# Memory attention with a gated feed-forward: two of four key and value chunks kept in q's buffers, phi's products in one piece beside P's last block

## The chip, the cores and the metric

One Trainium2 chip, one core. The metric is the device time of one launch in microseconds. All arithmetic that the text speaks of is in float32, or in float32 split into a high part (rounded to the chip's fp32r format) and a low part, so that most products are made three times: high by high, high by low, low by high.

## What is computed

Eight batches, eight heads, 576 tokens, head width 64, 32 memory slots per head; then a feed-forward network over all 4608 tokens.

```
a = softmax(phi, axis=2)                     # over the 576 tokens, phi[b, h, s, 32]
k_m = einsum('bhsm,bhsd->bhmd', a, k)        # 32 memory keys per head
v_m = einsum('bhsm,bhsd->bhmd', a, v)
attn = softmax(q @ k_m^T / 8, axis=-1)       # over the 32 slots
x = (attn @ v_m), heads side by side         # [4608, 512]
out = silu(x @ w_in) @ w_out                 # 512 -> 2048 -> 512
```

## The kernel before

**Blocks and slots.** The work goes batch by batch; a batch is called a block here, `b` from 0 to 7. `x @ w_in` is not made as such: attn (576 tokens by 256 head-and-slot pairs) is multiplied with P = v_m @ w_in, which has to be made anew for each block (`p_mm`, four pieces of 512 columns, `JW`). Blocks 2 to 7 run in 16 slots, `s = 8t + j`: token half `t` (288 tokens), and a pair `j` of 128-row chunks of the hidden layer. In each slot TensorE makes `h` (`ffn1s`, L836, twelve products into a PSUM tile of two banks), then small pieces of work for this or the next block (called by `run`), then the second layer's 21 products of the slot before (`st_step`, L875, into four banks `sum`). The second layer is a seven-product form of the 2 by 2 block product, for which `forms` builds sums of silu's output: ScalarE does silu (L850, and L852 for the 64 left columns) and the high parts (L854, L864), VectorE the sums (L855, L858, L859) and the low parts (L865, L866). In one slot of the first half VectorE does some of ScalarE's share (L861, L862), because ScalarE has an exp there.

**The next block's attention.** While block `b` runs, the pieces for block `n = b + 1` are put into slots by `ev(b, slot, fn, ...)`; `steady` does it for blocks 2 to 6. With `ex` = 4 in block 2 and 2 in blocks 3 to 6: `phi_exp` in slot `ex` (ScalarE, L319, with a load of the exp table before it and of the silu table behind it), `e_mm` (phi's products with keys and values, TensorE, L335: 16 products for each of four chunks of 128 tokens, and L345: 8 more and 8 more for the 64 tokens that are left), `e_tr`, then `s_all` (the scores, slot `ex + 5`, reads q). `e_mm` ends with the division by phi's sum: two additions and two reciprocals on VectorE (L353, L355), then one half of the result scaled on ScalarE (L359) and the other on VectorE (L361), both read from PSUM. In blocks 3 to 6, `p_mm` of P's third quarter stands in slot 0 and of its last quarter in slot 2; its result is read by ScalarE (`p_split`, L659) and VectorE (L661). In slot 3 there is also half of the softmax's scaling on VectorE (`s_norm`, L444), and in blocks of odd number the last three additions of the second layer of the block before (L916).

**PSUM.** Eight banks: four for `sum`, two for `h` (one tile, `bufs=1`, so that the next slot's `h` waits until everything that reads the tile is done), two for `bg`, which the small pieces use in turn. `h` fills columns 0 to 287 of each of its banks. `beside_h(w)` gives the `w` columns behind these, in the tile of the slot's own `h`.

**Homes in SBUF.** From block 3 on only two of the four chunk buffers `kv0` to `kv3` are left for keys and values, since the other two hold forms of `w_out`. So chunks 2 and 3 are loaded into `kv0` and `kv1` after the first half of `e_mm` has read these, and `e_mm` is made in two pieces, two slots apart (slots `ex + 1` and `ex + 3`). q has two buffers of its own, `q0` and `q1`, a little larger than a chunk (4608 to 4128 bytes a partition), filled by `load_q` and read by `s_all`.

**What sets the order.** TensorE runs in the order in which the code is written, and so does ScalarE from block 1 on. VectorE and the DMA queue (SyncE's, here SP) are ordered by a scheduler, under constraints: in a slot, VectorE's work that comes from `run` stands behind the slot's last `forms` instruction and behind `p_split`'s VectorE instruction (`behind`). DMAs are issued by SP in its order; each waits at the head of the queue until its buffer is free.

Of the kernel before, what the change touches and what calls it, by code (L numbers as in the profile page):

```python
# [10 lines left out]
F32 = mybir.dt.float32  # L11
# [8 lines left out]
P = 128  # L20
B, S, H, M, D = 8, 576, 8, 32, 64
HM = H * M
NR = H // 2
KVW = 2 * D + 1
# [3 lines left out]
JW = 512  # L28
# [6 lines left out]
FULLC = S // P  # L35
# [13 lines left out]
def attn_ffn_kernel(  # L49
# [11 lines left out]
    sb = ctx.enter_context(tc.tile_pool(name="sb", bufs=2))  # L61
# [53 lines left out]
    def bgtile():  # L115
        return ps.tile([P, 2, 512], F32, tag="bg", name="bg", bufs=1)
# [90 lines left out]
    at = [dict() for _ in range(B)]  # L207
    live = {}

    def banks(b):  # L210
        if b == 0:
            return [ps.tile([P, 512], F32, tag="acc", name=f"first{i}", bufs=NI) for i in range(2)]
        bg = bgtile()
        return [bg[:, 0], bg[:, 1]]

    def beside_h(w):

        return [live["h"][:, i, HALF : HALF + w] for i in range(2)]
# [10 lines left out]
    def load_kv(b, cs=range(FULLC)):  # L229
        queue = nc.scalar if b == 0 else None  # L230
        ts = at[b].setdefault("kv", [])
        for c in cs:
            n = c if b < 3 else c % 2
            t = sb.tile([P, 2, NR, KVW], F32, tag=f"kv{n}", name=f"kv{b}_{c}", bufs=1)
            load(t.rearrange("p g r f -> p (g r f)"), kv[b, :, c * KVC : (c + 1) * KVC], queue=queue)
            ts.append(t)
        if cs[0]:
            return
        t = sb.tile([P, NR, KVW], F32, tag="kr", name=f"kr{b}", bufs=1)
        load(t.rearrange("p r f -> p (r f)"), kv[b, :, FULLC * KVC :], queue=queue)  # L240
        at[b]["kr"] = t
# [6 lines left out]
    def rows(p):  # L248
        return slice(REST * p, REST * (p + 1))
# [75 lines left out]
    def e_mm(b, cs=range(FULLC)):  # L325
        e, er, kvt, kr = (at[b][k] for k in ("e", "er", "kv", "kr"))
        if cs[0] == 0:
            at[b]["pt"] = beside_h(KVW) if b == 2 else banks(b)
        pt = at[b]["pt"]
        turns = [(c, p) for c in cs for p in range(2)]  # L330
        if b == 0:
            turns.sort(key=lambda t: t[1])
        for c, p in turns:
            for r in range(NR):
                nc.tensor.matmul(  # L335
                    pt[p][M * r : M * (r + 1), :KVW],
                    e[:, p, c, M * r : M * (r + 1)],
                    kvt[c][:, p, r],
                    start=c == 0, stop=False, skip_group_check=True,
                )  # L340
        if cs[-1] != FULLC - 1:
            return
        for r in range(NR):
            for p in range(2):
                nc.tensor.matmul(  # L345
                    pt[p][M * r : M * (r + 1), :KVW],
                    er[rows(p), M * r : M * (r + 1)],
                    kr[rows(p), r],
                    start=False, stop=True, skip_group_check=True,
                )  # L350
        rs = [sb.tile([P, 1], F32, tag="rs", name="rs", bufs=2) for p in range(2)]
        for p in range(2):
            nc.vector.tensor_scalar(rs[p], pt[p][:, 2 * D : KVW], EPS, None, op0=ALU.add)  # L353
        for p in range(2):
            nc.vector.reciprocal(rs[p], rs[p])  # L355
        for p in range(2):
            src = pt[p][:, : 2 * D].rearrange("p (k d) -> p k d", k=2)
            if p == (b == 0):
                nc.scalar.activation(kvn[:, :, p], src, AF.Copy, scale=rs[p])  # L359
            else:  # L360
                last_kvn[:] = [nc.vector.tensor_scalar(kvn[:, :, p], src, rs[p], None, op0=ALU.mult)]  # L361
# [480 lines left out]
    def exp_slots(b):  # L842
        return () if b == B - 1 else (4, 11) if b == 2 else (2, 11)
# [128 lines left out]
    def ev(b, slot, fn, *a):  # L972
        events.setdefault((b, slot), []).append((fn, a))

    def steady(b, n):


        early = b > 2
        if not early:
            ev(b, 1, phi_max, n)  # L980
            for i in range(3):
                ev(b, 2, phi_fold, n, i)
            ev(b, 3, phi_sub, n)
        ex = exp_slots(b)[0]
        ev(b, 2, load_q, n, 1)
        ev(b, ex, phi_exp, n)
        ev(b, ex + 1, e_mm, n, range(2))
        ev(b, ex + 1, load_kv, n, range(2, FULLC))
        ev(b, ex + 3, e_mm, n, range(2, FULLC))
        ev(b, ex + 4, e_tr, n)  # L990
        ev(b, ex + 5, s_all, n)
        ev(b, 9 if early else 10, s_max, n, ALL)
        ev(b, 10, s_sub, n, ALL)
        ev(b, 11, s_exp, n, ALL)
        ev(b, 12 if early else 11, s_sum, n, ALL)
        ev(b, 13 if early else 12, s_norm, n, FIRST)
        turn = NFC + 3 if b % 2 else 14 if early else 13
        ev(b, turn, s_back, n, FIRST)
        ev(b, turn, s_high, n, FIRST)
        ev(b, turn, s_low, n, FIRST)  # L1000
        for k in range(3):
            ev(b, 10 + 2 * k, win_load, n, k)
        for k in range(2):
            ev(b, 13 + k, p_mm, n, k * JW, JW)
        m = n + 1
        if m < B:
            ev(b, ex + 3, load_kv, m, range(2))
            ev(b, ex + 3, load_phi, m)
            ev(b, ex + 5, load_q, m, 0)
            ev(b, 7 if early else 12, phi_max, m)  # L1010
            for i in range(3):
                ev(b, 11 + i if early else 13 + i, phi_fold, m, i, load)
            ev(b + 1, 1, phi_sub, m)

    for b in range(B):
        n = b + 1
        if b == 0:
            for j in range(2, DFF // CW):
                ev(b, 2 * j - 1.5, p_mm, b, j * CW, CW)
        elif b == 1:  # L1020
            ev(b, 0, win_save)
            for j in range(1, NJ):
                ev(b, 4 * j - 3, p_mm, b, j * JW, JW)
            for j in range(NP):
                ev(b, 1.5 * j + 2, w_forms, j, 0)
                ev(b, 1.5 * j + 2.5, w_forms, j, 1)
        else:
            ev(b, 0, win_load, b, 3)
            ev(b, 0 if b > 2 else 1, p_mm, b, 2 * JW, JW)
            if b > 2:  # L1030
                ev(b, 3, s_norm, b, SECOND)
                ev(b, 4, s_back, b, SECOND)
                ev(b, 4, s_high, b, SECOND)
                ev(b, 4, s_low, b, SECOND)
            ev(b, 2, p_mm, b, 3 * JW, JW)
            if n < B:
                steady(b, n)
            continue
        at_slot = (
            (4, 5, 6, 7.5, 9, 9.5, 11.5, 12.5, 13, 13.5, 14, 14) if b == 0  # L1040
            else (1, 2, 3, 5, 9, 10, 10, 11, 12, 13, 13, 14)
        )
        mx, sub, ex, em, tr, s0, s1, sx, se, ss, sn, sk = at_slot
        ev(b, mx, phi_max, n)
        if n == 1:
            ev(b, sub, phi_allmax, n, (0, 1), (0,))
            ev(b, sub + 0.5, phi_allmax, n, (0, 1), (1,))
        else:
            for i in range(3):
                ev(b, sub, phi_fold, n, i)  # L1050
        ev(b, sub + 0.5, phi_sub, n)
        ev(b, ex, phi_exp, n)
        ev(b, em, e_mm, n)
        ev(b, 14 if b == 0 else em + 1, load_kv, n + 1, range(FULLC if b == 0 else 2))
        ev(b, tr, e_tr, n)
        ev(b, em, load_q, n, 1)
        if n == 1:
            ev(b, s0, s_mm, n, 0)
            ev(b, s1, s_mm, n, 1)
        else:  # L1060
            ev(b, s0, s_all, n)
        ev(b, s1, load_q, n + 1, 0)
        ev(b, sx, s_max, n, ALL)
        ev(b, sx, s_sub, n, ALL)
        ev(b, se, s_exp, n, ALL)
        ev(b, ss, s_sum, n, ALL)
        ev(b, sn, s_norm, n, ALL)
        for u in (FIRST, SECOND) if n == 1 else (ALL,):
            ev(b, sk, s_back, n, ALL, u)
            ev(b, sk, s_high, n, ALL, u)  # L1070
        ev(b, sk, s_low, n, ALL)
        ev(b, sk, load_phi, n + 1)
        if b == 0:
            ev(b, 14, p_mm, n, 0, JW)
        else:
            for k in range(3):
                ev(b, 12 if k == 2 else 6 + k, win_load, n, k)
            for k in range(2):
                ev(b, 12 + 2 * k, p_mm, n, k * JW, JW)
# [154 lines left out]
    for b in range(B):  # L1234
# [3 lines left out]
        for s in range(NFC if b > 1 else 0):  # L1238
            t, j = divmod(s, NP)
# [5 lines left out]
        for fc in range(NFC if b < 2 else 0):  # L1245
# [7 lines left out]
            for part in range(2):  # L1253
# [3 lines left out]
                n = len(traced)  # L1257
                late = set()
                for fn, a in events.pop((b, fc + part / 2), []):
                    m = len(nc.cur_bb.bb.instructions)  # L1260
# [75 lines left out]
```

## Time and profile before

| | us |
|---|---|
| median of 3 runs | 684.99 (684.49 to 685.74) |
| the profiled execution's own time | 684.62 |
| its span, first to last instruction | 682.8 |
| TensorE busy in it | 672.2 (98%) |
| VectorE, ScalarE busy | 517.2, 368.9 |

The profile is of one execution. PE is TensorE's products, PEld its weight loads, DVE VectorE, ACT ScalarE, SP the DMA queue's engine. A row of the timeline has the start in us from the span's beginning, the duration, engine, source line, operation, output and input, how many instructions were merged, and in brackets the idle time before it with what ended that. The next instruction of an engine often starts before the end of the one before it; start to start is the better measure of what an instruction costs.

### The profile page before, as it was taken

What the parts mean: (1) busy time and instruction counts of PE and PEld (TensorE: products, weight loads), DVE (VectorE), ACT (ScalarE), POOL (GpSimd) and SP (SyncE); (2) the same over time, 40 slices, a digit from 0 to 9 for tenths busy, and PEclk for the clock granted to TensorE, in tenths of its full rate; (3) what the DMA queues carried; (4) which work ended last, traced back from release to release, by engine and by line L of the source; (5) the groups of instructions that cost most, each with busy time, mean ns of one, the idle gap of its engine ahead of it and who ended that gap; (6) DMA issues with size and microseconds to landing.
All of it is one profiled execution on the core that took longest, in us unless ns stands there. A gap on an engine that the chain in (4) does not pass through costs nothing.

```text
span 682.8 us, 14512 instructions
## 1 busy us (share of the span) xinstructions
PE 672.2 (98%) x5788; PEld 588.4 (86%) x5788; DVE 517.2 (76%) x1086; ACT 368.9 (54%) x678; POOL 0.7 (0%) x6
## 2 busy tenths in 40 slices
PE   8999999999999999999999999999999999999997
PEld 3578778787889997899988999899988999889996
DVE  4897899988938588868876678876886768867653
ACT  3878684533535455654644546564653636554541
POOL 0000000000000000000000000000000000000000
PEclk9999999999999999999999999999999999999999
DMA  9988975224360561253420435125431204210001
GB/s 342 363 330 281 328 285 206 85 86 160 105 208 3 175 225 63 78 178 132 169 93 16 151 127 179 69 95 182 156 114 43 79 2 155 95 46 17 32 1 47
DMA packets 37747, 93.92 MB, mean 138 GB/s; under 512 B 4656, under 2 KB 21168, under 8 KB 34096
## 3 DMA queue, kind: packets, MB, share of 16 engines
q1 hardware_dynamic: 36736, 90.22, 38.4%
q10 hardware_dynamic: 944, 2.77, 1.0%
q8 instruction: 46, 0.75, 0.5%
q14 instruction: 21, 0.17, 0.1%
HBM read 77.22 MB, written 15.73 MB: 136 GB/s over the span
## 4 chain that ended last, share of the span: by engine, by line
PE 80%; DVE 4%; issue 1%; DMA 1%; ACT 1%; ACTq 0%; DVEq 0%
PE sum L875 35%; PE h L836 22%; PE acc L728 6%; PE lsum L957 5%; PE bg L643 4%; PE h L683 3%; PE accleft L728 2%; PE bg L335 1%; PE bg L382 1%; DMA win<-win_saved 1%; DVE gparts L702 1%; DVE pm L661 0%; DVE aT L464 0%; DVE wo_lo L182 0%; DVE raw L178 0%
## 5 line engine op out<-in xcount | busy, mean ns | idle before, releaser
L836 PE MATMUL h<-aparts,pm 128*128 128x288 f32 x1152 | 169.0, 296 | 0.0
L836 PEld LDWEIGHTS h<-aparts,pm 128*128 128x128 f32 x1152 | 157.3, 188 | 1.4 <-issue 0.7
L850 ACT ACTIVATE gbuf<-h 128x512 f32<-128x512 f32 x96 | 57.3, 597 | 129.8 <-PE h L836 127.9
L875 PE MATMUL sum<-wo_hi,aparts 128*128 128x256 f32 x384 | 103.9, 293 | 0.0
L855 DVE TENSOR_TENSOR gbuf<-gbuf 128x256 f32<-128x256 f32 x96 | 40.5, 422 | 80.1 <-ACT gbuf L850 79.5
L875 PE MATMUL sum<-kept,aparts 128*128 128x256 f32 x576 | 100.1, 282 | 0.0
L875 PE MATMUL sum<-wo_lo,aparts 128*128 128x256 f32 x384 | 100.0, 282 | 0.0
L875 PEld LDWEIGHTS sum<-wo_hi,aparts 128*128 128x128 f32 x384 | 72.7, 189 | 19.2 <-ACT gleft L852 16.7
L864 ACT ACTIVATE aparts<-gbuf 128x512 fp32r<-128x512 f32 x86 | 54.4, 633 | 62.2 <-DVE gbuf L859 62.2
L728 PE MATMUL acc<-wo_hi,gparts 128*128 128x512 f32 x256 | 85.0, 397 | 0.2
L875 PEld LDWEIGHTS sum<-kept,aparts 128*128 128x128 f32 x576 | 82.5, 191 | 0.0
L866 DVE TENSOR_TENSOR gparts<-gbuf,aparts 128x512 fp32r<-128x512 f32 x86 | 59.4, 691 | 18.7 <-ACT aparts L864 18.7
L875 PE MATMUL sum<-wo_hi,gparts 128*128 128x256 f32 x384 | 73.2, 281 | 0.0
L875 PEld LDWEIGHTS sum<-wo_lo,aparts 128*128 128x128 f32 x384 | 73.1, 190 | 0.0
L875 PE MATMUL sum<-kept,gparts 128*128 128x256 f32 x288 | 65.5, 282 | 0.0
L728 PEld LDWEIGHTS acc<-wo_hi,gparts 128*128 128x128 f32 x256 | 47.6, 188 | 14.3 <-DVE t L818 1.7
L875 PEld LDWEIGHTS sum<-wo_hi,gparts 128*128 128x128 f32 x384 | 59.4, 190 | 0.0
L683 PEld LDWEIGHTS h<-aparts,pm 128*128 128x128 f32 x372 | 51.8, 188 | 6.5 <-issue 2.3
L683 PE MATMUL h<-aparts,pm 128*128 128x288 f32 x372 | 56.1, 299 | 0.4 <-ACT aparts L611 0.4
L854 ACT ACTIVATE aparts<-gbuf 128x384 fp32r<-128x384 f32 x96 | 50.4, 525 | 0.0
L728 PE MATMUL acc<-wo_lo,gparts 128*128 128x512 f32 x128 | 49.4, 393 | 0.3 <-DVE wo_lo L182 0.2
L875 PEld LDWEIGHTS sum<-kept,gparts 128*128 128x128 f32 x288 | 47.9, 190 | 0.0
(208 smaller groups left out, 954.2 us busy)
## 6 DMA issues: line engine op xcount, KB each, us to landing
win<-win_saved SPq DMA_DIRECT2D x24, 1024.0 KB, 5.1
kv<-in_kv SPq DMA_DIRECT2D x28, 516.0 KB, 4.7
q<-in_q SPq DMA_DIRECT2D x16, 576.0 KB, 4.7
raw<-in_w_in SPq DMA_DIRECT2D x14, 512.0 KB, 8.0
raw<-in_w_out SPq DMA_DIRECT2D x6, 1024.0 KB, 6.6
win_saved<-win SPq DMA_DIRECT2D x4, 1024.0 KB, 8.7
phi<-in_phi SPq DMA_DIRECT2D x7, 576.0 KB, 6.0
out<-oo SPq DMA_DIRECT2D x26, 128.0 KB, 2.3
```

The source lines that it names most:

```text
L335: nc.tensor.matmul(pt[p][M * r : M * (r + 1), :KVW], e[:, p, c, M * r : M * (r + 1)], kvt[c][:, p, r], start=c == 0, stop=False, skip_grou ...
L643: nc.tensor.matmul(bg[M * r : M * (r + 1), p, :w].rearrange("p (k f) -> p k f", f=P), kvT[D * p : D * (p + 1), 1, r], src[D * p : D * (p + ...
L683: nc.tensor.matmul(h[:, hf, :HALF], wt[:, p, fs], a[:, p, hf * HALF : (hf + 1) * HALF], start=n[hf] == 0, stop=n[hf] == 5, skip_group_chec ...
L728: nc.tensor.matmul(acc[key], gt[:, cs], wt[:, fc], start=fc == 0 and n == 0, stop=fc == NFC - 1 and n == 2)
L836: nc.tensor.matmul(h[:, i, :HALF], wt[:, p, f : f + P], a[:, p], start=n == 0, stop=n == 5)
L850: nc.scalar.activation(gbuf[:, :MAIN].rearrange("p (i f) -> p i f", i=2), h[:, :, :w], AF.Silu)
L854: nc.scalar.activation(hi[:, :3], g[:, 1:4], AF.Copy)
L855: nc.vector.tensor_tensor(g[:, 4:6], g[:, :1].broadcast_to([P, 2, P]), g[:, 1:3], op=ALU.subtract)
L864: nc.scalar.activation(hi[:, 3:], g[:, 4:], AF.Copy)
L866: last_split.append(nc.vector.tensor_tensor(lo[:, 3:], g[:, 4:], hi[:, 3:], op=ALU.subtract))
L875: nc.tensor.matmul(sums[bank][:, place * Q : (place + 1) * Q], gt[:, k], wt, start=bank not in begun, stop=True, skip_group_check=True,)
L957: nc.tensor.matmul(sums[k], part[gt][:, 2 * i + k], wt[:, fc], start=n == 0 and i == 0 and m == 0, stop=last and i == 1 and m == 2,)
```

## The change

Four edits, and what they move:

- **Homes.** From block 3 on, chunks 2 and 3 of keys and values go into q's buffers `q0` and `q1`, not into `kv0` and `kv1`. For a block `n` they are loaded after `s_all` has read q of the block before, and q itself is loaded after `e_mm` has read the chunks, in slot `ex + 2`.
- **One piece.** `e_mm` is made whole in slot `ex + 1`, no longer in slots `ex + 1` and `ex + 3`.
- **Where it is summed.** For blocks 4 to 7 (made during blocks 3 to 6) its sums go beside `h`, no longer into `bg`. For block 3 they stay in `bg`; for block 2 they were beside `h` before.
- **P's last quarter.** In blocks 3 to 6 `p_mm` of the last quarter moves from slot 2 to slot 3, the slot of `e_mm`.

```
-            n = c if b < 3 else c % 2
-            t = sb.tile([P, 2, NR, KVW], F32, tag=f"kv{n}", name=f"kv{b}_{c}", bufs=1)
+            tag = f"q{c - 2}" if b > 2 and c > 1 else f"kv{c}"
+            t = sb.tile([P, 2, NR, KVW], F32, tag=tag, name=f"kv{b}_{c}", bufs=1)
...
-            at[b]["pt"] = beside_h(KVW) if b == 2 else banks(b)
+            at[b]["pt"] = beside_h(KVW) if b in (2, *range(4, B)) else banks(b)
...
-        ev(b, 2, load_q, n, 1)
         ev(b, ex, phi_exp, n)
-        ev(b, ex + 1, e_mm, n, range(2))
-        ev(b, ex + 1, load_kv, n, range(2, FULLC))
-        ev(b, ex + 3, e_mm, n, range(2, FULLC))
+        ev(b, ex + 1, e_mm, n)
+        for hf in range(2):
+            ev(b, ex + 2, load_q, n, hf)
...
-            ev(b, ex + 5, load_q, m, 0)
+            ev(b, ex + 6, load_kv, m, range(2, FULLC))
...
-            ev(b, 2, p_mm, b, 3 * JW, JW)
+            ev(b, 3 if 2 < b < B - 1 else 2, p_mm, b, 3 * JW, JW)
...
-        ev(b, s1, load_q, n + 1, 0)
+        if b == 0:
+            ev(b, s1, load_q, n + 1, 0)
+        else:
+            ev(b, s1 + 1, load_kv, n + 1, range(2, FULLC))
```

The order in three places. First TensorE in block 4, slots 2 to 5, before: `h`, P's last quarter (L643), the second layer (L875, its first row only); a slot later half of phi's products; two slots later the other half.

```order
L836 MATMUL h<-aparts,pm 128x288 x12
L643 MATMUL bg<-win_3_4017,kvT_3371 32x512 x8
L875 MATMUL sum_4064<-wo_hi,aparts 128x256
...
L335 MATMUL bg<-kv_0_3319,phi_3325 32x129 x8
L335 MATMUL bg<-kv_1_3321,phi_3325 32x129 x8
...
L335 MATMUL bg<-kv_2_4186,phi_3325 32x129 x8
L335 MATMUL bg<-kv_3_4188,phi_3325 32x129 x8
L345 MATMUL bg<-kr_3323,phi_3325 32x129 x8
```

And now, all of it in slot 3:

```order
L836 MATMUL h<-aparts,pm 128x288 x12
L643 MATMUL bg<-win_3_4018,kvT_3370 32x512 x8
L335 MATMUL h<-kv_0_3318,phi_3324 32x129 x8
L335 MATMUL h<-kv_1_3320,phi_3324 32x129 x8
L335 MATMUL h<-kv_2_3497,phi_3324 32x129 x8
L335 MATMUL h<-kv_3_3499,phi_3324 32x129 x8
L345 MATMUL h<-kr_3322,phi_3324 32x129 x8
L875 MATMUL sum_4065<-wo_hi,aparts 128x256
```

Three pieces in three slots have become one, phi's products write to `h`'s tile, and slots 2 and 5 have no small piece left. (The rows count products; a product of float32 operands appears more than once in the trace.)

Second VectorE in block 3, from the end of slot 2 to slot 4, before:

```order
L862 TENSOR_TENSOR gparts<-gbuf,aparts 128x896
L661 TENSOR_TENSOR pm<-bg,pm 128x1024
L855 TENSOR_TENSOR gbuf<-gbuf 128x256
L858 TENSOR_TENSOR gbuf<-gbuf 128x128
L859 TENSOR_TENSOR gbuf<-gbuf 128x128
L865 TENSOR_TENSOR gparts<-gbuf,aparts 128x384
L866 TENSOR_TENSOR gparts<-gbuf,aparts 128x512
L444 TENSOR_TENSOR sc_2585<-sc_2585,ssm 128x2x288
L916 TENSOR_TENSOR x<-x,oo 128x256 x3
```

And now, from the middle of slot 3 to its end:

```order
L865 TENSOR_TENSOR gparts<-gbuf,aparts 128x384
L866 TENSOR_TENSOR gparts<-gbuf,aparts 128x512
L661 TENSOR_TENSOR pm<-bg,pm 128x1024
L444 TENSOR_TENSOR sc_2585<-sc_2585,ssm 128x2x288
L353 TENSOR_SCALAR rs<-h 128x1 x2
L916 TENSOR_TENSOR x<-x,oo 128x256
L355 RECIPROCAL rs<-rs 128x1 x2
L916 TENSOR_TENSOR x<-x,oo 128x256
L361 TENSOR_SCALAR kvn<-h,rs 128x2x64
L916 TENSOR_TENSOR x<-x,oo 128x256
```

P's low part (L661) has moved behind slot 3's own work, and the division (L353, L355, L361), which stood in slot 5, comes behind it and behind L444, with two of the three L916 among its rows. In blocks 4 and 6 the rows are the same without the L916.

Third ScalarE in block 4, from slot 2 (its L854) to slot 4 (the last row), before:

```order
L854 ACTIVATE aparts<-gbuf 128x384
L659 ACTIVATE pm<-bg 128x1024
L319 ACT_TABLE_LOAD
L319 ACTIVATE phi_3325<-phi_3325 128x1152
L850 ACT_TABLE_LOAD
L850 ACTIVATE gbuf<-h 128x512
L852 ACTIVATE gleft<-h 128x2x32
L854 ACTIVATE aparts<-gbuf 128x384
L864 ACTIVATE aparts<-gbuf 128x512
L850 ACTIVATE gbuf<-h 128x512
```

And now:

```order
L854 ACTIVATE aparts<-gbuf 128x384
L319 ACT_TABLE_LOAD
L319 ACTIVATE phi_3324<-phi_3324 128x1152
L850 ACT_TABLE_LOAD
L850 ACTIVATE gbuf<-h 128x512
L852 ACTIVATE gleft<-h 128x2x32
L854 ACTIVATE aparts<-gbuf 128x384
L864 ACTIVATE aparts<-gbuf 128x512
L659 ACTIVATE pm<-bg 128x1024
L359 ACTIVATE kvn<-h,rs 128x2x64
L850 ACTIVATE gbuf<-h 128x512
```

P's high part (L659) now stands behind slot 3's L864, and the division's L359 behind that, ahead of slot 4's silu.

In the built program the first product of slot 4's `h` waits for L361, and the first of phi's products for L852 of slot 3.

## The prediction

> **What bounds the kernel now.** The page first: how busy each engine is, and which engine the chain that ended last runs through.
>
> ```profile
> PE 672.2 (98%) x5788; PEld 588.4 (86%) x5788; DVE 517.2 (76%) x1086; ACT 368.9 (54%) x678; POOL 0.7 (0%) x6
> PE 80%; DVE 4%; issue 1%; DMA 1%; ACT 1%; ACTq 0%; DVEq 0%
> ```
>
> TensorE is the bound: it waits 682.8 - 672.2 = 10.6 us in all. So two things count: what a piece costs TensorE, and whether it has to wait for another engine. Both are read from the timeline of one block; I take block 4, slots 2 to 6, on TensorE.
>
> ```profile
> 370.16 1.74 PE L836 MATMUL h<-aparts,pm 128*128 128x288 f32 x12
> 371.83 1.09 PE L643 MATMUL bg<-win,kvT 64*32 64x512 f32 x16
> 372.85 0.39 PE L875 MATMUL sum<-wo_hi,aparts 128*128 128x256 f32 x1
> 375.45 1.74 PE L836 MATMUL h<-aparts,pm 128*128 128x288 f32 x12
> 377.12 1.09 PE L335 MATMUL bg<-kv,phi 128*32 128x129 f32 x32
> 378.14 0.38 PE L875 MATMUL sum<-wo_hi,aparts 128*128 128x256 f32 x1
> 380.75 1.76 PE L836 MATMUL h<-aparts,pm 128*128 128x288 f32 x12
> 384.87 1.75 PE L836 MATMUL h<-aparts,pm 128*128 128x288 f32 x12
> 386.55 1.09 PE L335 MATMUL bg<-kv,phi 128*32 128x129 f32 x32
> 387.57 0.45 PE L345 MATMUL bg<-kr,phi 64*32 64x129 f32 x16
> 387.95 0.39 PE L875 MATMUL sum<-wo_hi,aparts 128*128 128x256 f32 x1
> 390.54 1.76 PE L836 MATMUL h<-aparts,pm 128*128 128x288 f32 x12
> ```
>
> The starts of `h` divide it into slots. Slot 4 has no small piece: 384.87 - 380.75 = 4.12 us, the plain slot. Slot 2 with P's last quarter takes 5.29, slot 3 with the first half of phi's products 5.30, slot 5 with the second half 5.67. The four slots together take 390.54 - 370.16 = **20.38 us**. No piece waits here: each begins 1.67 or 1.68 after its `h`.
>
> **What the change saves on TensorE.** It joins three pieces. What they cost joined is in the trace already, in block 1, where the products of block 2 are made whole, beside `h`, and behind a piece of P:
>
> ```profile
> 131.52 1.09 PE L643 MATMUL bg<-win,kvT 64*32 64x512 f32 x16
> 132.54 1.97 PE L335 MATMUL h<-kv,phi 128*32 128x129 f32 x64
> 134.44 0.45 PE L345 MATMUL h<-kr,phi 64*32 64x129 f32 x16
> 134.82 0.50 PE L728 MATMUL acc<-wo_hi,gparts 128*128 128x512 f32 x1
> ```
>
> P's piece takes 1.02 (131.52 to 132.54), the products 1.90, the rest 0.38: 3.30 us to the next big product. In a joined slot 3 `h` therefore starts, then 1.67 until the piece, 3.30 for it, and 2.61 for the second layer (378.14 to 380.75): 7.58 us, when nothing waits. With slots 2, 4 and 5 plain that is 3 x 4.12 + 7.58 = 19.94, so 20.38 - 19.94 = 0.44 us saved in each of blocks 3 to 6. Block 3's own products, made in block 2, are joined without P's piece: two pieces of 1.18 (5.30 - 4.12) and 1.55 (5.67 - 4.12) become one of 1.67 + 1.90 + 0.38 + 2.61 - 4.12 = 2.44, a saving of 0.29; they stay in `bg`, whose next user comes three slots later, so nothing new waits there. All of it: 4 x 0.44 + 0.29 = **2.05 us**, if TensorE is never held up.
>
> **What it adds: slot 4's `h` now waits for the division.** The sums lie in the tile of slot 3's `h`, so the next `h` may not start before L361 has read them. On VectorE the division stands behind slot 3's own work, P's low part and L444 (the order above); before the change it was read out of `bg`, which nobody wanted for a slot. So a chain of ScalarE and VectorE now ends on TensorE's path, and I time it from rows.
>
> Where the chain begins: silu of slot 3. ScalarE has the exp in slot 2:
>
> ```profile
> 371.93 0.60 ACT L850 ACTIVATE gbuf<-h 128x512 f32<-128x512 f32 x1 [1.68 <-PE h L836]
> 372.56 0.52 ACT L854 ACTIVATE aparts<-gbuf 128x384 fp32r<-128x384 f32 x1
> 373.02 1.03 ACT L659 ACTIVATE pm<-bg 128x1024 fp32r<-128x1024 f32 x1
> 374.07 1.28 ACT L319 ACT_TABLE_LOAD   x1
> 375.36 1.17 ACT L319 ACTIVATE phi<-phi 128x1152 f32<-128x1152 f32 x1
> 376.55 1.28 ACT L850 ACT_TABLE_LOAD   x1
> 377.85 0.60 ACT L850 ACTIVATE gbuf<-h 128x512 f32<-128x512 f32 x1
> ```
>
> Before, slot 3's silu starts at 377.85, when the second table load is done. L659 leaves this place, so the first load can start when L854 ends (372.56 + 0.52 = 373.08) and not when L659 ends (374.05): 0.97 earlier, silu at 376.88. Counted from the start of slot 2's `h` (370.16) that is 6.72. TensorE is ahead of it: slot 3's `h` starts at 4.12 and could be read 1.77 later (371.93 - 370.16), at 5.89. So ScalarE is still 0.83 late.
>
> The Trainium skill, "ScalarE: Activation LUTs", section "What ACT_TABLE_LOAD costs", adds about 1380 ns of drain to each load of 1283 ns; by that, two drains would put silu 2.8 us later and the change some 11 us further to the slow side. The rows have the exp start 1.29 after its load starts, and silu 1.30, so no drain shows here and the sum goes by the rows.
>
> From silu to what follows P's low part: slot 0 of the same block has just these steps, one behind the other.
>
> ```profile
> 362.32 0.60 ACT L850 ACTIVATE gbuf<-h 128x512 f32<-128x512 f32 x1 [3.88 <-PE h L836]
> 364.06 0.63 ACT L864 ACTIVATE aparts<-gbuf 128x512 fp32r<-128x512 f32 x1 [0.59 <-DVE gbuf L859]
> 364.60 1.01 ACT L659 ACTIVATE pm<-bg 128x1024 fp32r<-128x1024 f32 x1
> 365.64 1.23 DVE L661 TENSOR_TENSOR pm<-bg,pm 128x1024 fp32r<-128x1024 f32 x1 [0.22 <-ACT pm L659]
> 366.78 0.41 DVE L963 TENSOR_TENSOR xl<-lsum,xl 128x256 f32<-128x256 f32 x1
> ```
>
> 366.78 - 362.32 = 4.46 from silu's start to the start of the next VectorE instruction, which is L444 now. L444 and the division, from block 3 and from slot 5 of block 4:
>
> ```profile
> 294.86 0.75 DVE L444 TENSOR_TENSOR sc<-sc,ssm 128x576 f32<-128x576 f32 x1
> 295.53 1.22 DVE L916 TENSOR_TENSOR x<-x,oo 128x256 f32<-128x256 f32 x3
> 390.21 0.22 DVE L353 TENSOR_SCALAR rs<-bg 128x1 f32<-128x1 f32 x2
> 390.39 0.23 DVE L355 RECIPROCAL rs<-rs 128x1 f32<-128x1 f32 x2
> 390.65 0.37 ACT L359 ACTIVATE kvn<-bg,rs 128x128 f32<-128x128 f32 x1 [1.08 <-DVE rs L355]
> 391.05 0.35 DVE L361 TENSOR_SCALAR kvn<-bg,rs 128x128 f32<-128x128 f32 x1 [0.43 <-ACT kvn L359]
> ```
>
> L444 0.67 (294.86 to 295.53); the division 1.19 (390.21 to 391.05 + 0.35 = 391.40). From VectorE's end to TensorE's start, a wait of the same kind in block 2:
>
> ```profile
> 265.79 1.19 DVE L661 TENSOR_TENSOR pm<-bg,pm 128x1024 fp32r<-128x1024 f32 x1
> 267.03 1.09 PE L643 MATMUL bg<-win,kvT 64*32 64x512 f32 x16 [1.43 <-DVE pm L661]
> ```
>
> 267.03 - 266.98 = 0.05. The sum, from the start of slot 2's `h`: 6.72 + 4.46 + 0.67 + 1.19 + 0.05 = **13.09** for slot 4's `h`. TensorE itself would be there at 4.12 + 7.58 = 11.70. So it waits 1.39 us in blocks 4 and 6. (Part of that may show at phi's products, which wait for slot 3's silu to have read `h`; it runs inside the same wait and ends nothing later.) The four slots now take 13.09 + 2 x 4.12 = 21.33, against 20.38: **0.95 longer**.
>
> In blocks 3 and 5 two L916 stand among the division's rows. One is between L353 and L355 and delays all behind it by a third of 1.22, 0.41; the other runs while ScalarE has L359 and VectorE would wait (0.43), so I count it at nothing. These blocks: 0.95 + 0.41 = **1.36 longer**.
>
> **The DMAs.** q's two loads move from early slots to behind phi's products, on SP behind one load of keys and values.
>
> ```profile
> q<-in_q SPq DMA_DIRECT2D x16, 576.0 KB, 4.7
> ```
>
> The products end at about 13.09 - 2.61 = 10.5 at the latest, and three such transfers one behind the other take 14.1: 24.6. The scores in slot 7 begin at 21.33 + 4.12 (slot 6) + 1.67 = 27.1. So 2.5 us are left even if nothing overlaps, and I count the loads at nothing; without that cover each us of lateness would be one us in each block. Chunks 2 and 3 are loaded behind the scores of the block before, over half a block ahead of need. The last quarter of P, now a slot later, is read from slot 6 on; its low part is done in slot 3.
>
> **The sum.** 2 x 0.95 + 2 x 1.36 - 0.29 = **+4.3 us**. The profiled execution took 684.62, of which 682.8 is span; it would take 688.9. The median of the runs is 684.99, 0.37 above it, so the forecast is **689.3 us**: slower by 0.6%. About 0.2%, 1.4 us, is what a measurement of this kernel can tell from no change.
>
> Bounds. Upward: the chain is counted with the overlaps seen in these rows (0.09 between L864 and L659, 0.09 behind L661, 0.08 behind L444); if some six steps don't overlap, each of four waits is 0.5 longer: +2.0, 691.3. Downward: the first rival.
>
> **Rivals.**
>
> 1. *The wait is there, but short.* If silu were not held by the table loads, it would start at 5.89, not 6.72, and each wait be 0.83 less: 0.12 longer in blocks 4 and 6, 0.53 in blocks 3 and 5, 1.3 - 0.29 = +1.0 in all: 686.0, which can't be told from no change. For it: TensorE's joined slot could start later than I think, and then the tables are loaded by the time. Against: ScalarE's rows are back to back from 372.56 to 377.85, and the order keeps both loads there. Chance 0.12.
> 2. *No wait: it is faster.* Price -2.05, 682.9. It decides at 11.70: VectorE has to have the division done 1.39 earlier than my chain. That takes rival 1's 0.83 and also L444 out of the way (0.67), for instance if VectorE's steps are quicker when phi's products are long done. For it: in block 1 the same joined piece beside `h` held nobody up. Against: there neither an exp nor L444 stood ahead of the division in its slot. Chance 0.07.
> 3. *q comes too late.* If other transfers take the DMA engines, and the second q lands 1 us after the scores could start, that adds 4 us: 693. For it: q had most of a block's time before. Against: 2.5 us to spare in a serial count, and transfers overlap. Chance 0.05.
>
> That the change doesn't do what it says I exclude: the order shows the pieces joined.
>
> **How the numbers follow.** My forecast has 0.76, with its own range from 687.3 (each of the four waits 0.5 shorter) to 691.3. The range of 8 in 10 goes down to rival 1 and leaves out rivals 2 and 3: 686.0 to 691.3. Slower by over 0.2%: the forecast, rival 3, and a part of rival 1, 0.84. Within 0.2%: most of rival 1, 0.08. Faster: rival 2 and a little beside, 0.08.
>
> **What would show it.** Right: in blocks 3 to 6 TensorE's row for slot 4's `h` carries an idle time released by L361's tile, kvn, or with part of it at L335; `h` of slot 2 to `h` of slot 4 takes 13.1 in block 4 (10.59 before) and 13.5 in block 3; `h` of slot 4 to that of slot 6 takes 8.2, where it was 9.79; L444 and L353 stand back to back behind L661; slot 3's silu starts 6.7 after slot 2's `h`. Wrong: no idle time at slot 4's `h` and 11.7 for slots 2 and 3 (rival 2); silu released by TensorE and not by a table load (rival 1); idle time at L382 released by the DMA of q (rival 3).

## The result and the profile after

| kernel | median, us | lowest to highest | ratio to before, 95% interval |
|---|---|---|---|
| before | 684.75 | 684.49 to 685.74 | |
| changed | 689.2 | 689.05 to 689.31 | 1.0064 (1.0053 to 1.0076) |

The change makes the kernel slower by 0.64%. The profiled execution took 689.25 us with a span of 687.5, 4.7 more than before's 682.8.

First the page of the changed kernel: the busy times of the engines, then the share of each engine in the chain that ended last.

```profile
PE 670.3 (97%) x5788; PEld 588.2 (86%) x5788; DVE 517.4 (75%) x1086; ACT 368.3 (54%) x678; POOL 0.7 (0%) x6
...
PE 73%; DVE 8%; ACT 3%; issue 2%; DMA 1%; DVEq 0%; ACTq 0%
```

TensorE is busy 1.9 us less than before (672.2), so the joining does save work. But it stands idle for 687.5 - 670.3 = 17.2 us, where it was 10.6. The chain has gone from TensorE (80% to 73%) to VectorE (4% to 8%) and ScalarE (1% to 3%). The waits of TensorE say for whom (total, how often, the longest):

```profile
PE h L335 <- ACT gleft L852: 3.0, 4, 0.8
PE h L836 <- DVE kvn L361: 2.8, 4, 0.8
```

Two new waits, each four times, once in each of blocks 3 to 6: 5.8 of the 6.6 us of added idle time; before's waits have neither. Both are for the tile of `h`. The other 0.8 lie near the start (0.4 more at L276, 0.4 at L335 of block 0), and yet block 2 begins only 0.13 later than before. The timeline of TensorE, block 3 and block 4:

```profile
283.73 1.74 PE L836 MATMUL h<-aparts,pm 128*128 128x288 f32 x12
...
291.36 1.97 PE L335 MATMUL h<-kv,phi 128*32 128x129 f32 x64 [0.79 <-ACT gleft L852]
...
297.24 1.86 PE L836 MATMUL h<-aparts,pm 128*128 128x288 f32 x12 [0.83 <-DVE kvn L361]
...
371.18 1.74 PE L836 MATMUL h<-aparts,pm 128*128 128x288 f32 x12
375.25 1.74 PE L836 MATMUL h<-aparts,pm 128*128 128x288 f32 x12
376.92 1.09 PE L643 MATMUL bg<-win,kvT 64*32 64x512 f32 x16
378.72 1.97 PE L335 MATMUL h<-kv,phi 128*32 128x129 f32 x64 [0.71 <-ACT gleft L852]
380.62 0.45 PE L345 MATMUL h<-kr,phi 64*32 64x129 f32 x16
384.33 1.86 PE L836 MATMUL h<-aparts,pm 128*128 128x288 f32 x12 [0.57 <-DVE kvn L361]
388.54 1.76 PE L836 MATMUL h<-aparts,pm 128*128 128x288 f32 x12
392.63 1.76 PE L836 MATMUL h<-aparts,pm 128*128 128x288 f32 x12
```

From the start of slot 2's `h` to that of slot 4's it is 384.33 - 371.18 = 13.15 in block 4 and 297.24 - 283.73 = 13.51 in block 3 (10.59 before in block 4). Slots 4 and 5 take 392.63 - 384.33 = 8.30 (9.79 before). In blocks 5 and 6 the same rows give 13.51 and 13.14.

Where the 4.7 us come from, by the starts of `h` in the two traces:

| stretch | before | after | difference | predicted |
|---|---|---|---|---|
| up to slot 0 of block 2 | 197.42 | 197.55 | +0.13 | 0 |
| block 2, slot 0 to block 3, slot 0 | 77.36 | 76.81 | -0.55 | -0.29 |
| slot 2 to slot 6, block 3 | 20.37 | 21.81 | +1.44 | +1.36 |
| the same, block 4 | 20.38 | 21.45 | +1.07 | +0.95 |
| the same, block 5 | 20.37 | 21.81 | +1.44 | +1.36 |
| the same, block 6 | 20.38 | 21.45 | +1.07 | +0.95 |
| all else | | | +0.1 | 0 |
| sum | | | +4.7 | +4.3 |

### The profile page after: what moved, and what is told of

It reads as the page before. It is cut to its first block, busy times and chain, and to the rows that moved or that the text cites. A ratio compares the mean times of both kernels' runs of the same rounds, so it can differ in the third digit from the quotient of the medians.

```text
span 687.5 us, 14515 instructions
## 1 busy us (share of the span) xinstructions
PE 670.3 (97%) x5788; PEld 588.2 (86%) x5788; DVE 517.4 (75%) x1086; ACT 368.3 (54%) x678; POOL 0.7 (0%) x6
## 4 chain that ended last, share of the span: by engine, by line
PE 73%; DVE 8%; ACT 3%; issue 2%; DMA 1%; DVEq 0%; ACTq 0%
PE sum L875 32%; PE h L836 20%; PE acc L728 6%; PE lsum L957 5%; PE h L683 3%; PE bg L643 3%; PE accleft L728 2%; DVE pm L661 1%; PE h L335 1%; ACT gbuf L850 1%; ACT L850 1%; PE bg L382 1%; DMA win<-win_saved 1%; ACT pm L659 1%; DVE gbuf L855 1%
## 5 line engine op out<-in xcount | busy, mean ns | idle before, releaser
L875 PE MATMUL sum<-wo_hi,aparts 128*128 128x256 f32 x384 | 103.0, 290 | 0.0
L875 PE MATMUL sum<-kept,aparts 128*128 128x256 f32 x576 | 100.1, 282 | 0.0
L875 PE MATMUL sum<-wo_lo,aparts 128*128 128x256 f32 x384 | 100.0, 282 | 0.0
L864 ACT ACTIVATE aparts<-gbuf 128x512 fp32r<-128x512 f32 x86 | 54.4, 633 | 62.5 <-DVE gbuf L859 62.5
L875 PEld LDWEIGHTS sum<-wo_hi,aparts 128*128 128x128 f32 x384 | 72.7, 189 | 14.9 <-ACT gleft L852 12.6
L875 PEld LDWEIGHTS sum<-kept,aparts 128*128 128x128 f32 x576 | 82.5, 191 | 0.0
L875 PE MATMUL sum<-wo_hi,gparts 128*128 128x256 f32 x384 | 73.2, 281 | 0.0
L875 PEld LDWEIGHTS sum<-wo_lo,aparts 128*128 128x128 f32 x384 | 73.1, 190 | 0.0
L875 PE MATMUL sum<-kept,gparts 128*128 128x256 f32 x288 | 65.5, 282 | 0.0
L875 PEld LDWEIGHTS sum<-wo_hi,gparts 128*128 128x128 f32 x384 | 59.4, 190 | 0.0
L854 ACT ACTIVATE aparts<-gbuf 128x384 fp32r<-128x384 f32 x96 | 50.4, 525 | 0.0
L875 PEld LDWEIGHTS sum<-kept,gparts 128*128 128x128 f32 x288 | 47.9, 190 | 0.0
```

The lines of the kernel that those rows point to most:

```text
L854: nc.scalar.activation(hi[:, :3], g[:, 1:4], AF.Copy)
L864: nc.scalar.activation(hi[:, 3:], g[:, 4:], AF.Copy)
L875: nc.tensor.matmul(sums[bank][:, place * Q : (place + 1) * Q], gt[:, k], wt, start=bank not in begun, stop=True, skip_group_check=True,)
```

## The experiments

The theory is the prediction's, with one thing added that the trace shows: `h`'s tile holds TensorE twice in the joined slot, once ahead of phi's products (until silu has read `h`), once behind the division. The rival that had to be told from it, besides late loads of q, is that the division's hold alone is the price, so that an earlier division gives all of the saving. Each edit is made to the changed kernel. Before, run on the same chips, took 684.89 us (beside the first four) and 684.68 (beside the other three); the ratios are to these. The changed kernel was not run beside them, so a difference to its 689.2 is good to about the 0.2 us by which before's medians differ.

| run | what | us | ratio to before, 95% interval |
|---|---|---|---|
| e1_bg | phi's products summed in `bg`, P's quarter in slot 2 | 682.91 | 0.9970 (0.9959 to 0.9982) |
| e2_norm | L444 a slot earlier | 686.5 | 1.0027 (1.0015 to 1.0039) |
| e3_div | division ahead of P's split and L444 | 685.28 | 1.0005 (0.9996 to 1.0013) |
| e4_p2 | P's quarter back in slot 2 | 688.97 | 1.0058 (1.0045 to 1.0072) |
| e5_rest | the L916 a slot earlier | 688.55 | 1.0057 (1.0041 to 1.0074) |
| e6_noexp | exp left out, so no table loads | 685.15 | 1.0006 (0.9997 to 1.0016) |
| e7_both | e3_div and e6_noexp together | 682.09 | 0.9959 (0.9944 to 0.9974) |

**e1_bg: the place beside `h` undone, and P's last quarter back in slot 2.** The homes in q's buffers and the one piece stay.

```
-            at[b]["pt"] = beside_h(KVW) if b in (2, *range(4, B)) else banks(b)
+            at[b]["pt"] = beside_h(KVW) if b == 2 else banks(b)
...
-            ev(b, 3 if 2 < b < B - 1 else 2, p_mm, b, 3 * JW, JW)
+            ev(b, 2, p_mm, b, 3 * JW, JW)
```

> The changed kernel with two of its edits undone: phi's products are summed in bg again and P's last quarter stands in slot 2 again. What stays: half of keys and values in q's homes, phi's products in one piece, q loaded late. Theory (the whole loss is TensorE's wait for h's tile): no wait is left in slots 3 and 4, only the joining remains, 4 x 0.29 in blocks 3 to 6 and 0.42 in block 2, so 684.8 - 1.6 = 683.2, faster than before. Rival (the late loads of q, or the homes, cost something by themselves): 684.8 or more, with idle time at the scores (L382) released by a DMA.

Measured 682.91: faster than both kernels. TensorE's timeline of this kernel, block 4:

```profile
369.27 1.74 PE L836 MATMUL h<-aparts,pm 128*128 128x288 f32 x12
...
376.23 1.97 PE L335 MATMUL bg<-kv,phi 128*32 128x129 f32 x64
378.13 0.45 PE L345 MATMUL bg<-kr,phi 64*32 64x129 f32 x16
...
381.12 1.76 PE L836 MATMUL h<-aparts,pm 128*128 128x288 f32 x12
...
389.32 1.76 PE L836 MATMUL h<-aparts,pm 128*128 128x288 f32 x12
```

No row carries an idle time, and the four slots take 389.32 - 369.27 = 20.05, 0.33 less than before. The late loads of q are the same here as in the change, and TensorE waits for none of them in blocks 3 to 6. So the loads cost nothing that shows, and the joining saves a little more than the 0.29 which the rows of block 1 give for it without P's piece. Two edits are undone here at once; e4_p2, which undoes P's place alone, keeps the loss, so the loss comes with the place beside `h`.

**e2_norm: one step out of the chain.** Half of the softmax's scaling stands in slot 2, not in slot 3.

```
-                ev(b, 3, s_norm, b, SECOND)
+                ev(b, 2 if b < B - 1 else 3, s_norm, b, SECOND)
```

> The changed kernel with L444 (half of the softmax's scaling) moved from slot 3 to slot 2 in blocks 3 to 6, where VectorE has room: nothing is left out. Theory (the chain runs through VectorE's order L661, L444, L353): 0.67 less wait in each of four blocks, 689.2 - 2.7 = 686.5; the wait at slot 4's h nearly gone in blocks 4 and 6. Rival (L444 runs while VectorE would wait for phi's products or for ScalarE anyway): 689.2.

Measured 686.5, 2.7 us below the change: four times 0.67, the price of L444 in the prediction's chain. TensorE's rows of slot 2's `h` and slot 4's, block 3 and block 4:

```profile
283.56 1.74 PE L836 MATMUL h<-aparts,pm 128*128 128x288 f32 x12
...
296.41 1.86 PE L836 MATMUL h<-aparts,pm 128*128 128x288 f32 x12 [0.16 <-DVE kvn L361]
...
370.34 1.74 PE L836 MATMUL h<-aparts,pm 128*128 128x288 f32 x12
...
382.82 1.86 PE L836 MATMUL h<-aparts,pm 128*128 128x288 f32 x12
```

Block 3 goes from 13.51 to 12.85 and block 4 from 13.15 to 12.48. In block 4 the division's wait is as good as gone, and yet TensorE is not at 11.70.

**e3_div: the division earlier.** In slot 3 the division comes right behind slot 3's own work on VectorE, ahead of P's high and low part and of L444; L359 stands ahead of L659 on ScalarE.

```
+        if slot == 3 and any(e[0] is e_mm for e in todo):
...
+            lb = p_mm(*late, False)
...
+            em[0](*em[1])
+            for i in list(nc.cur_bb.bb.instructions)[n:]:
+                if i.engine == DVE:
+                    behind(i, last_split[-1])
+            p_split(late[0], late[1], late[2], lb)
+            behind(last_p[0].ins, last_kvn[0])
```

> The changed kernel with the division (L353, L355, L359, L361) put ahead of P's high and low part (L659, L661) and of L444 on ScalarE and VectorE in blocks 3 to 6; the same work, the same order on TensorE. Theory A (there are two holds: slot 4's h waits for the division, and phi's products beside h wait until slot 3's silu has read h, as the trace's 0.71 before L335 shows): the second stays, TensorE starts slot 4's h 12.4 after slot 2's, 689.2 - 3.8 = 685.4, no better than before. Theory B (the prediction's second rival, in which only the division holds): 11.7 after slot 2's h, 682.9.

Measured 685.28. The division is done in time (in block 4 L361 ends at 381.04), and yet this is not the time of rival 2. TensorE's rows, block 4:

```profile
369.84 1.74 PE L836 MATMUL h<-aparts,pm 128*128 128x288 f32 x12
...
377.38 1.97 PE L335 MATMUL h<-kv,phi 128*32 128x129 f32 x64 [0.71 <-ACT gleft L852]
...
382.28 1.76 PE L836 MATMUL h<-aparts,pm 128*128 128x288 f32 x12
```

Slot 4's `h` waits for nobody, but comes at 382.28 - 369.84 = 12.44: the hold at phi's products is still there, 0.71, and now decides. In the changed kernel the division's wait ends later and covers it.

**e4_p2: P's last quarter back in slot 2.** Only phi's products stand in slot 3, beside `h`.

```
-            ev(b, 3 if 2 < b < B - 1 else 2, p_mm, b, 3 * JW, JW)
+            ev(b, 2, p_mm, b, 3 * JW, JW)
```

> The changed kernel with P's last quarter back in slot 2; phi's products stay in one piece beside h in slot 3. Theory A (two holds): silu of slot 3 is then held 0.97 longer by the table loads, and phi's products beside h wait for it; from slot 2's h to slot 4's 13.4 in all four blocks, 689.2 in all: P's place makes no difference. Theory B (only the division holds): 12.6 and 13.1, 687.5.

Measured 688.97, within 0.25 us of the change, although L659 and L661 have left the chain. ScalarE's timeline of this kernel, block 4, and behind it TensorE's:

```profile
373.95 1.03 ACT L659 ACTIVATE pm<-bg 128x1024 fp32r<-128x1024 f32 x1
374.99 1.28 ACT L319 ACT_TABLE_LOAD   x1
...
378.77 0.60 ACT L850 ACTIVATE gbuf<-h 128x512 f32<-128x512 f32 x1
```

```profile
371.08 1.74 PE L836 MATMUL h<-aparts,pm 128*128 128x288 f32 x12
...
379.53 1.97 PE L335 MATMUL h<-kv,phi 128*32 128x129 f32 x64 [1.42 <-ACT gleft L852]
```

L659 is back ahead of the first table load, silu of slot 3 comes 378.77 - 371.08 = 7.69 after slot 2's `h`, and the hold at phi's products has doubled to 1.42. Slot 4's `h` then comes at 384.43, 13.35, with no wait of its own. One hold has taken over the whole price of the two.

**e5_rest: the L916 out of the division.** In blocks 3 and 5 the last three additions stand in slot 2.

```
-        ev(*((b, 9) if t == 0 else (b, NFC + 1) if b % 2 else (b + 1, 3)), rest)
+        ev(*((b, 9) if t == 0 else (b, NFC + 1) if b % 2 else (b + 1, 2 if b < 6 else 3)), rest)
```

> The changed kernel with the three additions L916 of blocks 3 and 5 moved from slot 3 to slot 2, where VectorE has room; nothing is left out. Theory (one L916 delays the division in these two blocks): from slot 2's h to slot 4's 13.15 there as in blocks 4 and 6, where it is 13.51 now: 0.36 less in two blocks, 689.2 - 0.7 = 688.5. Rival (both L916 run while VectorE waits for ScalarE): 689.2.

Measured 688.55, 0.65 below the change. TensorE's rows, block 3:

```profile
283.65 1.74 PE L836 MATMUL h<-aparts,pm 128*128 128x288 f32 x12
...
296.88 1.86 PE L836 MATMUL h<-aparts,pm 128*128 128x288 f32 x12 [0.56 <-DVE kvn L361]
```

Slot 2's `h` to slot 4's takes 296.88 - 283.65 = 13.23 in block 3, where the change has 13.51, so L916 costs 0.28 in each of two blocks.

**e6_noexp: silu not held by table loads.** The exp of phi is a copy for blocks 4 to 7, so ScalarE keeps silu's table; this kernel leaves a part of the computation out.

```
-            nc.scalar.activation(at[b]["et"], at[b]["et"], AF.Exp)
+            nc.scalar.activation(at[b]["et"], at[b]["et"], AF.Copy if b > 3 else AF.Exp)
```

> The changed kernel with the exp of phi replaced by a copy for blocks 4 to 7, so that no table is loaded in slots 2 and 3 of blocks 3 to 6; this part of the computation is left out. Theory (silu of slot 3 is held by the two table loads, and both holds with it): silu starts 5.9 after slot 2's h and not 6.7, no wait is left at phi's products, and the division's chain ends at 12.3: 0.87 less in each of four blocks, 689.2 - 3.5 = 685.7. Rival (silu is held by h, the loads are hidden): 689.2.

Measured 685.15. This gives rival 1 its condition: no table load holds silu. ScalarE's rows, block 4, and TensorE's:

```profile
372.77 1.15 ACT L319 ACTIVATE phi<-phi 128x1152 f32<-128x1152 f32 x1
375.78 0.60 ACT L850 ACTIVATE gbuf<-h 128x512 f32<-128x512 f32 x1 [1.86 <-PE h L836]
```

```profile
369.93 1.74 PE L836 MATMUL h<-aparts,pm 128*128 128x288 f32 x12
...
376.69 1.97 PE L335 MATMUL h<-kv,phi 128*32 128x129 f32 x64
...
382.15 1.86 PE L836 MATMUL h<-aparts,pm 128*128 128x288 f32 x12 [0.41 <-DVE kvn L361]
```

Silu of slot 3 starts 5.85 after slot 2's `h` and is released by TensorE; phi's products run without a wait; only the division's wait is left, and slot 4's `h` comes at 12.22.

**e7_both: both holds gone.** The edits of e3_div and e6_noexp; the exp is left out here too.

> The two together: the division ahead of P's parts and of L444, and the exp of phi replaced by a copy for blocks 4 to 7; this part of the computation is left out. Theory (the two holds are all that the change costs): slot 4's h starts 11.7 after slot 2's, with no idle time, the price of the prediction's second rival: 1.4 and 1.8 less than the changed kernel in blocks 4, 6 and 3, 5, and 0.1 less after it: 689.2 - 6.8 = 682.4. Rival (something else in the change costs time as well): 684 or more.

Measured 682.09. TensorE's rows, block 4:

```profile
369.05 1.74 PE L836 MATMUL h<-aparts,pm 128*128 128x288 f32 x12
...
380.70 1.76 PE L836 MATMUL h<-aparts,pm 128*128 128x288 f32 x12
...
388.90 1.76 PE L836 MATMUL h<-aparts,pm 128*128 128x288 f32 x12
```

No wait is left, slot 4's `h` comes 380.70 - 369.05 = 11.65 after slot 2's, and the four slots take 19.85. Each of the two edits alone brings the kernel to within 0.2% of before (685.28, 685.15), 3.9 and 4.05 us below the change, and the two together 7.1. That is not the sum of both, since three paths end at slot 4's `h` and the longest counts: TensorE's own (11.65), phi's products behind silu (12.44) and the division (13.15). The earlier division takes the third below the second, the earlier silu shortens the second and the third by 0.9, and the first stays.

## Why the prediction was right

It gave 689.3 us for a kernel that took 689.2. The mechanism came as forecast; that the total is only 0.1 off is in part luck. The span grew by 4.7 where the sum had 4.3, and before's median is 684.75 here, 0.24 below the 684.99 from which the forecast started. Its steps, one by one.

**The chain that sets slot 4's `h`: right, piece by piece.** ScalarE's timeline of the changed kernel, block 4, and then VectorE's:

```profile
374.13 1.28 ACT L319 ACT_TABLE_LOAD   x1
375.42 1.17 ACT L319 ACTIVATE phi<-phi 128x1152 f32<-128x1152 f32 x1
376.66 1.28 ACT L850 ACT_TABLE_LOAD   x1
377.95 0.60 ACT L850 ACTIVATE gbuf<-h 128x512 f32<-128x512 f32 x1
378.45 0.22 ACT L852 ACTIVATE gleft<-h 128x64 f32<-128x64 f32 x1
```

```profile
381.27 1.23 DVE L661 TENSOR_TENSOR pm<-bg,pm 128x1024 fp32r<-128x1024 f32 x1 [0.23 <-ACT pm L659]
382.41 0.75 DVE L444 TENSOR_TENSOR sc<-sc,ssm 128x576 f32<-128x576 f32 x1
383.08 0.22 DVE L353 TENSOR_SCALAR rs<-h 128x1 f32<-128x1 f32 x2
383.26 0.23 DVE L355 RECIPROCAL rs<-rs 128x1 f32<-128x1 f32 x2
383.92 0.35 DVE L361 TENSOR_SCALAR kvn<-h,rs 128x128 f32<-128x128 f32 x1 [0.43 <-ACT kvn L359]
```

| piece | predicted | block 4 |
|---|---|---|
| slot 2's `h` to silu of slot 3 | 6.72 | 377.95 - 371.18 = 6.77 |
| silu to L444 | 4.46 | 382.41 - 377.95 = 4.46 |
| L444 | 0.67 | 0.67 |
| the division | 1.19 | 384.27 - 383.08 = 1.19 |
| to `h` | 0.05 | 384.33 - 384.27 = 0.06 |
| sum | 13.09 | 13.15 |

L444 and L353 stand back to back, as said. e2_norm, e5_rest, e6_noexp and e3_div each take one piece away, and the time falls by it until the other hold decides.

**Silu and the table loads: right.** Silu is released by the table load, not by TensorE, and e6_noexp shows what it is worth: silu comes 0.92 earlier (6.77 to 5.85) and the time falls by 4.05 us. Exp and silu each start 1.29 after their load begins. The Trainium skill, "ScalarE: Activation LUTs", section "What ACT_TABLE_LOAD costs", adds a drain of about 1380 ns to each load; no row of this kernel shows it either.

**Odd blocks: right in the sum, two pieces wrong.** 13.50 was predicted and 13.51 came. VectorE's rows of the changed kernel in block 3:

```profile
295.71 0.22 DVE L353 TENSOR_SCALAR rs<-h 128x1 f32<-128x1 f32 x2
295.85 0.42 DVE L916 TENSOR_TENSOR x<-x,oo 128x256 f32<-128x256 f32 x1
296.18 0.22 DVE L355 RECIPROCAL rs<-rs 128x1 f32<-128x1 f32 x2
296.31 0.41 DVE L916 TENSOR_TENSOR x<-x,oo 128x256 f32<-128x256 f32 x1
296.83 0.35 DVE L361 TENSOR_SCALAR kvn<-h,rs 128x128 f32<-128x128 f32 x1
```

L353 to L355 takes 0.47 where block 4 has 0.18: the first L916 costs 0.29, not 0.41, and the second nothing. The remaining part is earlier, in ScalarE's rows of block 3:

```profile
289.30 1.28 ACT L850 ACT_TABLE_LOAD   x1 [0.15 <-DVE gparts L862]
290.59 0.60 ACT L850 ACTIVATE gbuf<-h 128x512 f32<-128x512 f32 x1
```

Here silu starts 290.59 - 283.73 = 6.86 after slot 2's `h`, 0.14 later than the 6.72 of the prediction and 0.09 later than in block 4, since its table load first waits 0.15 for VectorE's L862. Two errors of about 0.1 cancelled; e5_rest, which takes away 0.28 and not 0.41, tells them apart.

**Mis-sized terms of the sum.** The four slots grew by 0.08 more than predicted in odd blocks and 0.12 in even ones, 0.4 in all. Most of that is the slot behind the wait: slot 4 takes 388.54 - 384.33 = 4.21, where the prediction had a plain 4.12, four times 0.09. The saving in block 2 was 0.55, not 0.29: before, the two slots with half pieces and the one between them took 15.22 (220.54 to 235.76), not the 5.30 + 4.12 + 5.67 = 15.09 of the prediction, and the joined ones 14.76, as predicted but for 0.04; the last 0.09 lies elsewhere in the block. And 0.13 came ahead of block 2, which the sum did not have. In the traces of all nine kernels block 2 begins between 197.26 and 197.71, before's at 197.42, so 0.13 can't be told from the scatter of single executions.

**"It runs inside the same wait and ends nothing later": true for the forecast, and short of the whole.** The wait at phi's products (0.71) does lie inside the path that the division ends. But it is a second floor: with it TensorE reaches slot 4's `h` at 12.44 (e3_div), not at the 11.70 which the prediction gave as TensorE's own time. So of the 1.39 us that the prediction calls the wait, only 13.15 - 12.44 = 0.71 can be had from the division. Rival 2 named both of its conditions, silu's 0.83 and the rest; its example of quicker VectorE steps would not have been enough. e7_both, which meets both, has 11.65 and 682.09, against 11.70 and 682.9 in the prediction; rival 1's 13.09 - 0.83 = 12.26 is 12.22 in e6_noexp.

**The two holds are of one kind.** The Trainium skill, "PSUM — Partial Sum Buffer", section "PSUM bank collisions raise a hardware error", says that two engines may not touch one bank and group of partitions at once, whatever the addresses, and that the compiler makes one wait for the other. The rows agree as far as they go: phi's products wait for silu's read of other columns of the tile (0.71), and the next `h` for the division's read (0.57). That `h` and the sums use different columns frees nobody. No run here tells a rule on banks from one on whole tiles. The 0.43 that L361 waits for L359 is not of this kind: in the code the two read different banks of the tile, and both write `kvn`; they wait so before the change too (0.43).

**q late (rival 3): no.** The trace of after shows no wait for q in blocks 3 to 6, and e1_bg with the same loads is the fastest kernel here that leaves nothing out. q's loads do take longer, 6.1 us at the median against 4.7.

## What to carry to other kernels

A sum put into the free columns of a single-buffered PSUM tile takes on both of that tile's holds: it may not start until the tile's readers are done, and the tile's next writer may not start until the sum's own readers are; price both, as a maximum of paths and not as a sum. Joining pieces on TensorE (0.33 us a block for two pieces in e1_bg, 0.53 for three in e7_both) pays if the joined piece keeps banks of its own: e1_bg does so and takes 682.91 us, 0.3% less than before, where the change, which joins beside `h`, loses 0.64%. When one wait of two on a path is taken away, look in the trace for the one that it covered before counting on the gain.

## What was not expected of the hardware

An `h` that had to wait at its start takes 0.10 longer: 1.86 us behind a wait (384.33) and 1.76 without (388.54), and its slot 4.21 against 4.11 (382.28 to 386.39 in e3_div, the same place with no wait there). A very short wait has the same effect: in e2_norm's block 4 slot 4's `h` starts 0.30 behind the last products ahead of it, where 0.24 is usual (388.30 to 388.54 in the changed kernel), and takes 1.86. It is not so for every group of products: phi's take 1.97 with a wait of 0.71 and 1.97 without one (e1_bg). One difference stands in the rows: the weight loads of an `h` that doesn't wait start 0.12 ahead of its first product (388.42 and 388.54), those of an `h` that waited start with it (both 384.33), and those of phi's products start with the first product in either case (both 378.72, both 376.23). That this is the cause is not shown.

And joining the pieces is worth a little more than block 1's rows said: without any wait the four slots take 19.85 (e7_both), where 19.94 was worked out.
